# Three edits in the opening stage of a retention and mixture-of-experts kernel: two weight splits on another engine, a scaling moved up in a queue, a score step moved down

## The chip, the cores and the metric

The kernel runs on one core of a Trainium2 chip. The metric is the device time of one execution in microseconds (us). Five engines take part, each with its own queue that it works through in order: TensorE (PE in the rows; its weight loads are PEld), VectorE (DVE), ScalarE (ACT), GpSimd (POOL) and SyncE (SP), which only issues DMAs here.

## The reference

```python
scores = scale * np.matmul(q, k.transpose(0, 1, 3, 2))      # 4 batches, 8 heads, 576 tokens, 64 wide
gamma = 1.0 - 2.0 ** (-5.0 - np.arange(H))
Dmat = np.where(rel >= 0, gamma[:, None, None] ** rel, 0.0) # rel = i - j
x = np.matmul(scores * Dmat, v)                             # retention, no softmax
h = x @ w_in                                                # 2304 tokens, 512 -> 2048
x = (h / (1.0 + np.exp(-1.702 * h))) @ w_out                # dense layer, 2048 -> 512
# then a router picks one of 8 experts per token by cosine similarity,
# and the token goes through relu(x @ w1[e]) @ w2[e], times its gate
```

All arrays are float32. `w_in` and `w_out` arrive as 64-bit numbers and are turned into float32 in the kernel.

## The kernel before, in words

**Retention (functions inside `attention_`).** The 32 pairs of a batch and a head are taken two heads at a time: 16 "rows" bp, four to a batch (bp 0 to 3 are batch 0, bp 8 to 11 batch 2). The first 512 tokens of a row are worked in four chunks of 128, with a carried state between chunks; the last 64 tokens are the row's "end" and are worked by functions of their own. The tables `tb`/`tbs` hold powers of gamma. `decay` scales a row's keys in place (L335, on DVE for the rows of `DVE_ROWS = (0, 2, 7, 8, 9)`, else on POOL). For batches 2 and 3 it also scales the row's queries in place on POOL (L339) and, for the batch's first row, the end queries of all its four rows in one instruction (L342, tile `more`). `state` makes the carried state (PE L351, then ACT L352), `scores` and `masks` the chunk scores (PE L313, DVE L329), `scores_end` the scores of the ends of the rows in its list (PE L319, then DVE L322), `carried`, `ends_out` and `chunk` the outputs (PE L365, L373 and L375, L383), `keep` and `kept_out` move outputs from PSUM (DVE L404 for odd rows of the last two batches), `make_lows` splits the results of batches 0 and 1 for the next stage (POOL L433).

The rows are walked in groups, `[0], [1, 2], [3, 4], ... [13, 14], [15]`, numbered k = 0 to 8. In iteration k, `rows` is the group itself, `nxt` the next one, whose states and scores are prepared, and `then` the one after it, whose keys are scaled. Before the change the scaling of `then` stands at the head of the iteration for rows on POOL and at its tail for rows of `DVE_ROWS`; a row's query scaling stands with its key scaling. So the end queries of batch 2 (first row 8) are scaled at the tail of iteration 2, and those of batch 3 (first row 12) in the middle of the head of iteration 4. PE reads the end queries of row 8 in `scores_end(nxt)` of iteration 3.

**Weights of the dense layer (`convert`).** A unit u is the weights of 128 hidden columns; there are 16. For each, ACT takes the magnitude (L168), DVE works on bits (L181, L183, L191, L196), ACT makes the high half (L171) and a subtraction makes the low half (`low(u)`, L175): on POOL for units 0 and 1, on DVE for the others. PE's matmuls use both halves. `convert` is a generator: each `yield` gives the cost of the instruction in front of it, and `pull(us)` runs the generator until its budget is used up, an overdraft being taken from the next pull:

```python
while us > 0 and k < len(bg):
    cost = next(bg[k], None)
    ...
        us -= cost
debt.append(min(us, 0.0))
```

During retention there are nine pulls of 0.9 (one in iteration 5, three each in 6 and 7, two in 8), then one of 2.4, then one of 2.6 inside each step of the dense layer's first two blocks. The order of DVE's queue follows from these budgets alone.

**Dense layer.** Blocks of 384 tokens go through the 16 units; blocks 0 and 1 are interleaved, so unit f is used in steps 2f and 2f + 1. A step i is `layer1` (PE L566, 12 matmuls into one of two PSUM tiles `h`), then `swish`: ACT L597, DVE L599, ACT L600, the step's pull, DVE L604; and `layer2` (PE L577, 9 matmuls) of step i - 2. L599 frees the PSUM tile, so `layer1` of step i + 2 waits for L599 of step i, and the second matmul of `layer2` for L604.

After the two blocks come four more dense blocks with the router in between, then the experts. `fill_slots` (POOL L1003 and L1004) stands in POOL's queue behind retention and behind the two low halves.

Of the kernel before, what the change touches and what calls it, by code (L numbers as in the profile page):

```python
# [10 lines left out]
F32 = mybir.dt.float32  # L11
# [4 lines left out]
ALU = mybir.AluOpType  # L16

P = 128
B, H, S, HD = 4, 8, 576, 64
NPAIR = H // 2  # L20
NCH = 4
TAIL = S - NCH * P
# [35 lines left out]
AQ, AK, AV, AW = NCH * P, 2 * NCH * P, 3 * NCH * P, 4 * NCH * P  # L58
TQ, TV, TAW = TAIL, 2 * TAIL, 3 * TAIL
# [18 lines left out]
def retention_moe_kernel(  # L78
# [18 lines left out]
    PE, ACT, DVE, POOL, SP = nc.tensor, nc.scalar, nc.vector, nc.gpsimd, nc.sync  # L97
# [6 lines left out]
    c = pool.tile([P, CU], F32, name="c")  # L104
# [17 lines left out]
    units = {}  # L122
# [4 lines left out]
    def new_unit(u):  # L127
        s = u if u < NF1 else (u - NF1) % RING
        units[u] = unit_tile(f"unit{u}", [P, 2, 1024], F32R, HELD + s)
        return units[u]  # L130
# [14 lines left out]
    def load_due():  # L145

        if st.get("loaded"):
            while due:
                load_wd(due.pop(0))

    def flush(*keys):
        for k in keys or list(later):
            if k in later:
                later.pop(k)()

    def convert():

        words = [pool.tile([P, 1024], I32, tag="stg", bufs=2, name=f"ca{k}") for k in range(2)]

        def word(u):  # L160

            if u == 3 and len(words) == 2:
                t = pool.tile([P, 2, 1024], I32, tag="tab", bufs=2, name="ca")
                words.extend((t[:, 0, :], t[:, 1, :]))
            return words[u % 2 if u < 3 else (2, 3, 1, 0)[(u - 3) % 4]]

        def magnitude(u):
            ACT.activation(word(u).bitcast(F32), stg["d", u][:, :, 1].bitcast(F32), AF.Abs)  # L168

        def high(u):  # L170
            ACT.copy(new_unit(u)[:, 0, :], word(u).bitcast(F32))  # L171

        def low(u):
            flush(("high", u))
            (POOL if u < 2 else DVE).tensor_tensor(units[u][:, 1, :], word(u).bitcast(F32), units[u][:, 0, :].bitcast(F32), ALU.subtract)  # L175

        magnitude(0)
        for u in range(NF1):
            a = word(u)
            flush(("mag", u))  # L180
            DVE.tensor_scalar(a.bitcast(F32), a.bitcast(F32), 2.0**-15, CLAMP_HI, ALU.max, ALU.min)  # L181
            yield 0.67
            DVE.tensor_scalar(a, a, 3, 0x3FFFFFF8, ALU.logical_shift_left, ALU.bitwise_and)  # L183
            yield 0.67
            d = stg.pop(("d", u))
            if 0 < u < 4:
                low(u - 1)
                yield 1.22 if u > 2 else 0.1
            if u + 1 < NF1:
                later["mag", u + 1] = lambda u=u: magnitude(u + 1)  # L190
            DVE.scalar_tensor_tensor(a, d[:, :, 1], -0x40000000, a, ALU.bitwise_and, ALU.bitwise_or)  # L191
            yield 1.22
            if u > 3:
                low(u - 1)
                yield 1.22
            DVE.scalar_tensor_tensor(a, d[:, :, 0], 29, a, ALU.logical_shift_right, ALU.bitwise_or)  # L196
            if u + NWD < NF1:
                due.append(u + NWD)
                load_due()
            later["high", u] = lambda u=u: high(u)  # L200
            yield 1.22
        low(u)
        yield 0.1

# [35 lines left out]
    def attention_(psum):  # L240
# [5 lines left out]
        row = [place[i] for i in range(NBUF)] + [place[i] for i in order[2:]]  # L246
# [3 lines left out]
        tbs = tb[:, TX:n].rearrange("p (n w) -> p n w", w=TW)  # L250
# [3 lines left out]
        tl = [t[:, NPAIR * TAW * i : NPAIR * TAW * (i + 1)].rearrange("p (n w) -> p n w", w=TAW) for t in (ends, more) for i in range(2)]  # L254
# [42 lines left out]
        def idle(n, w=64):  # L297
            for _ in range(n):
                PE.matmul(warm[:w, :P], ones[:, :w], ones, start=True, stop=True)
# [15 lines left out]
        def scores_end(rows):  # L315
            for k, bp in enumerate(rows):
                e = tl[bp // NPAIR][:, bp % NPAIR, :]
                for r in heads:
                    PE.matmul(sct[r, TAIL * k : TAIL * (k + 1)], e[r, :TQ], e[r, TQ:TV], start=True, stop=True)  # L319
            for k, bp in enumerate(rows):  # L320
                g = tbs[:, bp % NPAIR, TE : TE + 1]
                DVE.scalar_tensor_tensor(pre[bp % 4], sct[:, TAIL * k : TAIL * (k + 1)], g, tri_end, ALU.mult, ALU.mult)  # L322
# [8 lines left out]
        def decay(bp):  # L331
            if bp < NBP:
                kd = row[bp][:, AK:AV].rearrange("p (c e) -> p c e", e=HD)
                dec = tbs[:, bp % NPAIR, TK:TS]
                (DVE if bp in DVE_ROWS else POOL).tensor_tensor(kd, kd, dec.unsqueeze(2).to_broadcast(kd.shape), ALU.mult)  # L335
                b, pair = divmod(bp, NPAIR)
                if b > 1:
                    qd = row[bp][:, AQ:AK].rearrange("p (c q) -> p c q", q=P)
                    POOL.tensor_tensor(qd, qd, tbs[:, pair, :P].unsqueeze(1).to_broadcast(qd.shape), ALU.mult)  # L339
                    if pair == 0:  # L340
                        qe = tl[b][:, :, TQ:TV]
                        POOL.tensor_tensor(qe, qe, tbs[:, :, :TAIL], ALU.mult)  # L342

        def state(bp, ch):
            t = row[bp]
# [12 lines left out]
        def carried(bp):  # L358
            t, kv = row[bp], kvs[bp % 2]
            new_out(bp)  # L360
            for ch in range(1, NCH):
                for r in heads:
                    o = st["o", bp][r, P * ch : P * (ch + 1)]
                    first = ch == 1 and bp > 0
                    PE.matmul(o, kv[r, 64 * (ch - 1) : 64 * ch], t[r, AQ + P * ch : AQ + P * (ch + 1)], start=first, stop=True, skip_group_check=not first)  # L365
# [28 lines left out]
        def keep_end(bp):  # L394
            x, o = kept_in(bp)[:, NCH * P :], st.pop(("ot", bp))
            if bp // NPAIR > 1:
                ACT.copy(x, o)
            else:
                DVE.tensor_tensor(x, o, tbs[:, bp % NPAIR, :TAIL], ALU.mult)
# [31 lines left out]
        def make_lows(b):  # L431
            while lows and lows[0][0] <= b:
                POOL.tensor_tensor(*lows.pop(0)[1:], ALU.subtract)  # L433
# [27 lines left out]
        for k, rows in enumerate(groups):  # L461
            nxt, then = (groups + [[], []])[k + 1 : k + 3]
            for bp in then:
                if bp > 2 and bp not in DVE_ROWS:
                    decay(bp)
            for bp in rows:
                carried(bp)
            ends_out(rows)
            scores_end(nxt)
            for bp in rows:  # L470
                keep_end(bp)
            if k > 5:
                yield False
            if nxt:
                scores(nxt[0])
            if k == 0:
                decay(2)
                masks(nxt[0])
                keep(0)
                for ch in range(NCH):  # L480
                    for bp in nxt:
                        state(bp, ch)
                    if ch == 1:
                        scores(nxt[1])
                        masks(nxt[1])
                    else:
                        idle(4)
            else:
                if nxt:
                    masks(nxt[0])  # L490
                values(rows, nxt)
            for bp in rows:
                if ("o", bp) in st:
                    kept_out(bp)
            make_lows(0 if k < 6 else 1)
            for bp in rows:
                if bp in WD_AT:
                    load_wd(WD_AT.index(bp))
                if bp in follows:
                    load(follows[bp])  # L500
                if follows.get(bp) == NBP - 1:

                    st["loaded"] = True
                    SP.dma_start(c[:, :CET], cst[:, :CET])
                    SP.dma_start(c[:, CET : CET + KD * E], embt)
                    uf = pool.tile([P, P], F32, tag="cvb", bufs=1, name="uf")
                    SP.dma_start(uf, cst[:, CU:CSL])
                    load_due()
            if k > 5:
                yield True  # L510
            for bp in nxt[1:] if k else []:
                scores(bp)
                masks(bp)
            for bp in then:
                if bp > 2 and bp in DVE_ROWS:
                    decay(bp)
            if 4 < k < 8:
                yield True
# [627 lines left out]
    for i in range(nd - 1):  # L1146
# [22 lines left out]
        if i >= LAG:  # L1169
            dense2(i - LAG)  # L1170
            u = i - LAG - (nd - NF1)
# [203 lines left out]
```

## Time and profile before

| | |
|---|---|
| median of three runs | 726.77 us (725.94 to 726.87) |
| the profiled execution | 727.92 us, of which the span shown is 726.1 us |
| PE busy | 706.9 us, 97% of the span |
| DVE busy | 458.3 us, 63% |
| ACT busy | 307.2 us, 42% |
| POOL busy | 207.2 us, 29% |

The span runs from the first to the last instruction in the record; 1.8 us of the execution lie around it. PE is busy nearly throughout, so the time is found in the places where it is not, or where its clock is not full.

### The profile page before, as it was taken

Reading aid. Unit: us, or ns where it says so; the run is one execution under the profiler, and the core shown is the slowest. Engines: PE = TensorE matmul, PEld = TensorE weight load, DVE = VectorE, ACT = ScalarE, POOL = GpSimd, SP = SyncE. Lnnn points to the kernel's source line nnn. Section 1 sums busy time; section 2 is a strip of 40 time slices with the busy share of each in tenths; the row PEclk is TensorE's granted clock in tenths of the full one; section 3 lists DMA queues with packets and bytes.
Section 4 is the critical chain, followed back from the end, with each engine's and each line's share of the span. In section 5 each row is a group of like instructions: output and inputs, shape, how many; then the busy total and the mean of one; then the engine's idle time right before and its main releaser. Section 6 shows DMA issues by size and latency. Waiting matters only on the chain. (4 is left out here: it accounts for less than half of the span.)

```text
span 726.1 us, 13167 instructions
## 1 busy us (share of the span) xinstructions
PE 706.9 (97%) x4903; PEld 657.3 (91%) x4903; DVE 458.3 (63%) x1034; ACT 307.2 (42%) x598; POOL 207.2 (29%) x195
## 2 busy tenths in 40 slices
PE   8999799999999999999999999999999999999995
PEld 7888699899899899899999889989999999999994
DVE  3668998888535887665477368656563553563561
ACT  2435354454345332332332244343444545555542
POOL 0673100000000221220111101224346546566553
PEclk9999899999999999999999999999999999999998
DMA  8997999000310013200400221144678879987861
GB/s 335 417 365 287 387 346 354 11 1 1 112 66 2 0 48 85 87 1 1 132 0 1 88 88 58 59 142 126 205 207 261 225 239 259 245 255 241 265 186 62
DMA packets 53156, 113.41 MB, mean 156 GB/s; under 512 B 8146, under 2 KB 29138, under 8 KB 48992
## 3 DMA queue, kind: packets, MB, share of 16 engines
q1 hardware_dynamic: 49744, 102.55, 43.6%
q0 software_dynamic: 3200, 9.46, 3.7%
q8 instruction: 39, 0.64, 0.4%
q10 hardware_dynamic: 144, 0.52, 0.2%
q14 instruction: 29, 0.24, 0.1%
HBM read 84.67 MB, written 28.17 MB: 155 GB/s over the span
## 5 line engine op out<-in xcount | busy, mean ns | idle before, releaser
L566 PE MATMUL h<-x,unit 128*128 128x384 f32 x1152 | 219.4, 339 | 3.5 <-DVE g0t L599 3.5
L566 PEld LDWEIGHTS h<-x,unit 128*128 128x128 f32 x1152 | 206.2, 189 | 12.2 <-DVE g0t L599 3.8
L222 POOL TENSOR_TENSOR unit<-we,unit 128x512 fp32r<-128x512 f32 x64 | 102.3, 1605 | 118.7 <-ACT unit L220 99.3
L566 PE MATMUL eh<-xt,unit 128*128 128x336 f32 (+6 forms) x672 | 102.1, 300 | 0.3 <-DVE eg54l L611 0.2
L566 PEld LDWEIGHTS eh<-xt,unit 128*128 128x128 f32 x672 | 95.4, 188 | 0.9 <-DVE eg54l L611 0.5
L221 DVE TENSOR_TENSOR unit<-we,unit 128x512 fp32r<-128x512 f32 x64 | 56.1, 877 | 59.2 <-ACT unit L220 58.7
L673 DVE CUSTOM_DVE_ANT_0 dj<-xr,en 128x512 bf16<-128x512 f32 x120 | 78.0, 696 | 0.0
L220 ACT CAST unit<-we 128x1024 fp32r<-128x1024 f32 x64 | 66.8, 1046 | 25.5 <-DMA we<-we 25.4
L639 POOL TENSOR_TENSOR enrm<-scr,c 128x8 f32<-128x8 f32 x1 | 1.7, 1687 | 142.0 <-ACT ej L644 142.0
L352 ACT ACTIVATE ends<-s,tb 128x64 f32<-128x64 f32 x64 | 17.4, 311 | 36.8 <-PE s L351 33.8
L616 POOL DMA_INDIRECT out<-y,idx x24 | 24.0, 1000 | 31.2 <-ACT y L839 20.6
L616 POOL DMA_INDIRECT xs<-xr,slot x18 | 19.4, 1077 | 39.1 <-DVE xr L748 35.7
L733 POOL TENSOR_TENSOR cum<-cum,oh_all 128x8 bf16<-128x8 bf16 x18 | 4.8, 265 | 67.2 <-PE rk L726 52.4
L539 POOL TENSOR_TENSOR x<-x0s,x 128x768 fp32r<-128x768 f32 x3 | 6.1, 2031 | 48.6 <-ACT x L538 48.6
L175 DVE TENSOR_TENSOR unit<-ca,unit 128x1024 fp32r<-128x1024 f32 x14 | 17.1, 1220 | 4.3 <-ACT unit L171 4.3
L191 DVE SCALAR_TENSOR_TENSOR ca<-wd,ca 128x1024 int32<-128x1024 int32 x16 | 19.6, 1222 | 0.3
L329 DVE SCALAR_TENSOR_TENSOR pr<-sc,tb 128x512 f32<-128x512 f32 x22 | 15.5, 745 | 6.7 <-PE sc L313 6.7
L196 DVE SCALAR_TENSOR_TENSOR ca<-wd,ca 128x1024 int32<-128x1024 int32 x16 | 19.5, 1219 | 0.1
L313 PE MATMUL sc<-row 64*128 64x128 f32 x256 | 18.8, 285 | 0.6 <-DMA row<-att 0.6
L839 ACT ACTIVATE y<-y,gate 128x512 f32<-128x512 f32 (+7 forms) x21 | 14.3, 713 | 10.9 <-DMA y<-yd 9.7
L335 POOL TENSOR_TENSOR row<-row,tb 128x512 f32<-128x512 f32 x11 | 11.5, 1044 | 24.8 <-DMA row<-att 13.2
L168 ACT ACTIVATE ca<-wd 128x1024 f32<-128x1024 f32 x16 | 18.3, 1147 | 0.0
(1312 smaller groups left out, 1543.7 us busy)
## 6 DMA issues: line engine op xcount, KB each, us to landing
we<-we SPq DMA_DIRECT2D x64, 512.0 KB, 4.5
wd<-wd SPq DMA_DIRECT2D x16, 1024.0 KB, 11.1
row<-att SPq DMA_DIRECT2D x14, 1024.0 KB, 13.2
xs<-fill SPq DMA_DIRECT2D x22, 257.0 KB, 10.8
xrow<-xr SPq DMA_DIRECT2D x18, 257.0 KB, 4.0
y<-yd SPq DMA_DIRECT2D x7, 512.0 KB, 4.7
x0d<-x0f SPq DMA_DIRECT2D x4, 768.0 KB, 11.3
x0s<-x0d SPq DMA_DIRECT2D x8, 384.0 KB, 6.7
```

The source lines that it names most:

```text
L168: ACT.activation(word(u).bitcast(F32), stg["d", u][:, :, 1].bitcast(F32), AF.Abs)
L175: (POOL if u < 2 else DVE).tensor_tensor(units[u][:, 1, :], word(u).bitcast(F32), units[u][:, 0, :].bitcast(F32), ALU.subtract)
L191: DVE.scalar_tensor_tensor(a, d[:, :, 1], -0x40000000, a, ALU.bitwise_and, ALU.bitwise_or)
L196: DVE.scalar_tensor_tensor(a, d[:, :, 0], 29, a, ALU.logical_shift_right, ALU.bitwise_or)
L220: ACT.copy(w[:, 0, :], t)
L221: DVE.tensor_tensor(w[:, 1, :512], t[:, :512], w[:, 0, :512].bitcast(F32), ALU.subtract)
L222: POOL.tensor_tensor(w[:, 1, 512:], t[:, 512:], w[:, 0, 512:].bitcast(F32), ALU.subtract)
L313: PE.matmul(scs[j][:, P * ch : P * (ch + 1)], t[r, P * ch : P * (ch + 1)], t[r, AQ + P * ch : AQ + P * (ch + 1)], start=True, stop=True)
L352: ACT.activation(kvs[bp % 2][:, 64 * ch : 64 * ch + 64], s, AF.Copy, scale=tbs[:, bp % NPAIR, TS + ch : TS + ch + 1])
L566: PE.matmul(h, w[:, a, P * dc : P * (dc + 1)], xt[:, b, dc, :n], start=k == 0, stop=k == len(terms) - 1)
L616: i = POOL.indirect_dma_start(out=dst[:, :], out_offset=bass.IndirectOffsetOnAxis(ap=rows, axis=0), in_=src, in_offset=None, bounds_check= ...
L673: DVE.tensor_tensor_reduce(junk, r[:, :D], en[e // 4][:, e % 4, :], 1.0, 0.0, ALU.mult, ALU.add, dots[:, E * k + e : E * k + e + 1])
```

## The change

The low halves of units 0 and 1 move from POOL to DVE, and their cost for the pulls becomes 1.22 in place of 0.1. `decay` is cut into three: key scaling stays where it was, the end queries of a batch are scaled at the head of the iteration before all else, and a row's queries are scaled at the head of the iteration whichever engine scales its keys. `scores_end(nxt)` of iteration 0 (rows 1 and 2) moves from in front of that iteration's scores and states to behind them.

```diff
         def low(u):
             flush(("high", u))
-            (POOL if u < 2 else DVE).tensor_tensor(units[u][:, 1, :], word(u).bitcast(F32), units[u][:, 0, :].bitcast(F32), ALU.subtract)
+            DVE.tensor_tensor(units[u][:, 1, :], word(u).bitcast(F32), units[u][:, 0, :].bitcast(F32), ALU.subtract)
...
             if 0 < u < 4:
                 low(u - 1)
-                yield 1.22 if u > 2 else 0.1
+                yield 1.22
...
                 (DVE if bp in DVE_ROWS else POOL).tensor_tensor(kd, kd, dec.unsqueeze(2).to_broadcast(kd.shape), ALU.mult)
-                b, pair = divmod(bp, NPAIR)
-                if b > 1:
-                    qd = row[bp][:, AQ:AK].rearrange("p (c q) -> p c q", q=P)
-                    POOL.tensor_tensor(qd, qd, tbs[:, pair, :P].unsqueeze(1).to_broadcast(qd.shape), ALU.mult)
-                    if pair == 0:
-                        qe = tl[b][:, :, TQ:TV]
-                        POOL.tensor_tensor(qe, qe, tbs[:, :, :TAIL], ALU.mult)
+
+        def decay_ends(bp):
+            b, pair = divmod(bp, NPAIR)
+            if b > 1 and pair == 0:
+                qe = tl[b][:, :, TQ:TV]
+                POOL.tensor_tensor(qe, qe, tbs[:, :, :TAIL], ALU.mult)
+
+        def decay_queries(bp):
+            b, pair = divmod(bp, NPAIR)
+            if b > 1:
+                qd = row[bp][:, AQ:AK].rearrange("p (c q) -> p c q", q=P)
+                POOL.tensor_tensor(qd, qd, tbs[:, pair, :P].unsqueeze(1).to_broadcast(qd.shape), ALU.mult)
...
             for bp in then:
+                decay_ends(bp)
+            for bp in then:
                 if bp > 2 and bp not in DVE_ROWS:
                     decay(bp)
+                decay_queries(bp)
             for bp in rows:
                 carried(bp)
             ends_out(rows)
-            scores_end(nxt)
+            if k:
+                scores_end(nxt)
...
                         idle(4)
+                scores_end(nxt)
             else:
```

## Rows read from the trace of the kernel before

**Rows 1.** Windows: stretch; its length, busy PE, PEld, DVE, ACT, POOL; granted clock; DMA.
```profile
38.60:41.90 3.30, 3.30 (x40) 3.30 (x42) 1.95 (x3) 1.06 (x4) 3.30 (x4) 0.50 1.02 422
84.00:89.00 5.00, 4.96 (x14) 4.35 (x15) 3.37 (x5) 2.88 (x4) 0.00 (x0) 0.50 1.01 426
150.00:200.00 50.00, 50.00 (x253) 45.28 (x252) 36.34 (x49) 21.43 (x34) 0.00 (x0) 1.00 0.13 44
```

**Rows 2.** PE's timeline, iterations 2 to 4: start, length, instruction, idle before.
```profile
27.76 0.40 PE L319 MATMUL sct<-ends 64*64 64x64 f32 x8
...
35.17 0.28 PE L319 MATMUL sct<-ends 64*64 64x64 f32 x4
37.15 0.33 PE L319 MATMUL sct<-more 64*64 64x64 f32 x4 [1.69 <-POOL more L342]
...
38.50 0.68 PE L351 MATMUL s<-row 128*64 128x64 f32 x8
...
46.11 0.40 PE L319 MATMUL sct<-more 64*64 64x64 f32 x8
```

**Rows 3.** POOL's timeline from 33 to 37 us.
```profile
33.22 1.55 POOL L433 TENSOR_TENSOR x<-x,x 128x384 fp32r<-128x384 f32 x2 [2.63 <-ACT x L423]
...
35.96 1.13 POOL L342 TENSOR_TENSOR more<-more,tb 128x256 f32<-128x256 f32 x1
```

**Rows 4.** SP's issue of batch 2's ends, and that DMA's time to landing.
```profile
15.55 0.33 SPq L269 DMA_DIRECT2D more<-tails  x1
...
more<-tails SPq DMA_DIRECT2D x1, 384.0 KB, 14.4
```

**Rows 5.** DVE's timeline: key scaling of row 2, and of rows 7 and 8.
```profile
13.49 0.68 DVE L335 TENSOR_TENSOR row<-row,tb 128x512 f32<-128x512 f32 x1
...
34.77 2.87 DVE L335 TENSOR_TENSOR row<-row,tb 128x512 f32<-128x512 f32 x2
```

**Rows 6.** Timeline of POOL and PE in iteration 1, row 4.
```profile
20.81 1.04 POOL L335 TENSOR_TENSOR row<-row,tb 128x512 f32<-128x512 f32 x1 [1.65 <-DMA row<-att]
...
21.91 0.34 PE L351 MATMUL s<-row 128*64 128x64 f32 x4 [0.26 <-POOL row L335]
```

**Rows 7.** PE's timeline from 74 to 104 us.
```profile
74.03 0.87 PE L365 MATMUL ao<-row,ends 64*64 64x128 f32 x12 [1.63 <-DVE x0f L404]
...
76.08 4.46 PE L566 MATMUL h<-x,unit 128*128 128x384 f32 x24
84.03 4.21 PE L566 MATMUL h<-x,unit 128*128 128x384 f32 x12 [3.48 <-DVE g0t L599]
...
91.12 2.25 PE L566 MATMUL h<-x,unit 128*128 128x384 f32 x12
...
103.66 2.27 PE L566 MATMUL h<-x,unit 128*128 128x384 f32 x12
```

**Rows 8.** POOL's timeline: the low halves of units 0 and 1.
```profile
68.42 2.35 POOL L175 TENSOR_TENSOR unit<-ca,unit 128x1024 fp32r<-128x1024 f32 x1 [9.08 <-ACT unit L171]
77.58 2.39 POOL L175 TENSOR_TENSOR unit<-ca,unit 128x1024 fp32r<-128x1024 f32 x1 [6.81 <-ACT unit L171]
```

**Rows 9.** DVE's and ACT's timelines from 68 to 88 us.
```profile
68.86 2.47 DVE L181 TENSOR_SCALAR ca<-ca 128x1024 f32<-128x1024 f32 x1
...
73.29 0.68 DVE L404 COPY x0f<-ao 128x512 f32<-128x512 f32 x1
...
77.62 3.37 DVE L183 TENSOR_SCALAR ca<-ca 128x1024 int32<-128x1024 int32 x1
...
83.42 0.55 DVE L599 SCALAR_TENSOR_TENSOR g0t<-g0t,h 128x384 f32<-128x384 f32 x1
...
84.42 1.14 ACT L168 ACTIVATE ca<-wd 128x1024 f32<-128x1024 f32 x1
85.60 0.69 DVE L181 TENSOR_SCALAR ca<-ca 128x1024 f32<-128x1024 f32 x1 [1.63 <-ACT ca L168]
...
86.93 1.22 DVE L175 TENSOR_TENSOR unit<-ca,unit 128x1024 fp32r<-128x1024 f32 x1
```

## The prediction

> **What bounds the kernel now.** I began with the busy times and the waits of PE, because PE is busy for nearly the whole span and its idle time is short enough to list. Behind the first hundred microseconds it hardly waits: from 150 to 200 us it is busy throughout, at full clock, with DVE and ACT well below and DMAs at 0.13 [rows 1]. Steps there follow each other at PE's pace, 4.18 us for a `layer1` and a `layer2` (three of them from 91.12 to 103.66 [rows 7]). So I take the rest of the kernel as rigid: what the opening saves arrives whole at the end. PE's timeline then shows three waits from 30 to 91 us: 1.69 for the scaled end queries of batch 2 [rows 2], 1.63 for a PSUM tile that DVE empties, and 3.48 for DVE's L599 of step 0 [rows 7]. The windows add that two of the three are paid twice. [...] I then followed each wait to its engine, in the timelines of POOL and DVE.
>
> **End queries earlier.** An ordinary iteration lasts 7.41 us from end scores to end scores (27.76 to 35.17), the one with the wait 10.94 (35.17 to 46.11) [rows 2]: 3.53 is lost, 1.69 in the wait and 1.84 in slow matmuls behind it. The wait is for L342, which runs on POOL from 35.96 to 37.09, behind two low halves and the query scaling L339 [rows 3]. After the change it is first in iteration 2. POOL is free from 30.59 (33.22 less the 2.63 idle [rows 3]) and the data landed at 29.95 (15.55 + 14.4 [rows 4]), so L342 should end near 31.8, 3.6 us before PE asks at 35.46. What is now queued behind it on POOL is the query scaling of row 8, then the two low halves of L433; those are read in the dense layer, some 40 us later. In iteration 4 L342 of batch 3 goes ahead of the scaling of rows 11 and 12, 1.13 us that their readers, an iteration later, don't notice. SP's queue has no DMA moved.
>
> What is late next is DVE's key scaling of rows 7 and 8. Two such instructions took 2.87 us, from 34.77, just when POOL went from L433 to L339 and L342; one alone took 0.68 [rows 5]. They would end at 37.64 again if POOL now worked beside them for as long (the rest of L433, then the queries of row 9), at 36.13 if it didn't. PE asks for row 8's states at about 36.8 (38.50 less 1.69 [rows 2]). So between 0 and 0.84 us of the 3.53 comes back as a new wait; I take 0.3, because less of POOL's work is left there than before. Gain 3.2, between 2.7 and 3.5.
>
> [...]
>
> **End scores of rows 1 and 2 behind their states.** These matmuls wait for a DMA in iteration 0, and PE can now go on with scores meanwhile. But in iteration 1 PE already waits 0.26 us for POOL's scaling of row 4, which starts when that row's DMA lands, at 20.81 [rows 6]. No edit brings that DMA forward, so what iteration 0 saves is spent there. Gain 0; at most the 0.26 that stands there now, and no loss, since DVE's part of the end scores is read only after the 24 matmuls of `carried`.
>
> **Low halves on DVE.** POOL's two splits take 2.35 and 2.39 us [rows 8], and beside each a DVE instruction is stretched: L181 to 2.47 and L183 to 3.37 [rows 9], where L181 at 85.60 takes 0.69. That is 1.78 and 2.68 of DVE's time, 4.46 together, against 2 x 1.22 (the same split on DVE, 86.93 [rows 9]) that the edit adds. POOL's fill instructions stood behind the second split and lengthened L183 with it; nothing now holds them back from the idle time after L433.
>
> The pulls also shift. With 1.22 for 0.1, the budgets of 0.9 hand out: end of iteration 5, L181 and L183 of unit 0; iteration 6, L191 and L196; iteration 7, L181 and L183 of unit 1, then low(0) with an overdraft that gives L191 to iteration 8's first pull and L196 to its second; the pull of 2.4, L181, L183 of unit 2 and low(1); step 0, L191 and L196; step 1, L181 and L183 of unit 3 and low(2). Conversion thus runs about one pull behind the old order.
>
> Now in the clock of the trace shown, before the 3.2 is taken off. (1) L404 of row 13 starts at 73.29 - 1.78 = 71.51 and ends at 72.19. PE is ready at 74.03 - 1.63 = 72.40, so that wait goes: 1.63. (2) `layer1` of step 0 starts at 76.08 - 1.63 = 74.45; steps 0 and 1 take 4.18, so PE is free at 78.63. (3) DVE behind 72.19 does low(0) 1.22, L191 and L196 2.43 (as from 80.99, the end of L183, to 83.42 [rows 9]), L404 of row 15 0.68, a small cast put at 0.2, L181 and L183 1.38, low(1) 1.22, L599 0.55: it ends at 79.87. PE waits 1.24 there, in place of 84.03 - 80.26 = 3.77. (4) `layer1` of step 2 ends at 81.96; L604 of step 0 ends at 79.87 + 2.43 + 0.55 = 82.85, so `layer2` of step 0 waits after its first matmul and ends at 84.7. (5) `layer1` of step 3 ends at 86.8. DVE has L599 of step 1 at 83.4, then ACT copies (0.5, estimated like L599) and takes the magnitude (1.14 [rows 9]) before L181 can start at 85.05; L183, low(2) and L604 put the end at 88.2. `layer2` of step 1 waits again and ends at 90.1.
>
> Before, that point (`layer1` of step 4) was 91.12 + 4.18 = 95.30, so the sum saves 5.2. The clock's part lies in it: from 84.03 to 91.12 a step took 7.09 in place of 4.18 [rows 7], and I hold that waits of about 1 us with full steps between leave the clock up, as the 1.63 at 72.40 did (24 matmuls behind it in 4.46, against 12 in 4.21 behind the 3.48 [rows 7]). Recorded lengths on DVE overlap: L181, L183 and the next start fit into 1.33 (85.60 to 86.93) where two lengths make 1.38, and more between independent ones; over a dozen instructions up to 1 us. With all of it the saving is 6.2. I take 6.0. The ceiling is a PE that never waits: 72.40 plus 2.05 plus six times 2.09 is 86.99, a saving of 8.3. From there on DVE needs 0.55 + 2.6 + 0.55 = 3.7 per step against PE's 4.18, and catches up.
>
> **Sum.** 3.2 + 0 + 6.0 = 9.2 us. The profiled execution took 727.92, so it would be 718.7 (span 716.9). The median of the runs is 1.15 below that execution; from 726.77 the forecast is 717.6.
>
> **Rivals.** (a) The clock falls again behind one of the three new waits (near 79, 82 or 87 us). For it: a wait of 1.69 was followed by a fall, one of 1.63 was not, so length alone doesn't decide. Against: none of mine is longer than 1.24. Price: the excess of that step, 7.09 - 4.18 = 2.9: 720.5. [...] (b) DVE's long L181 and L183 are not POOL's doing. Then the 4.46 stay, 2.44 are added on DVE, L599 of step 0 ends later and the low halves lose 2.4: 726.8 - 3.2 + 2.4 = 726.0. Against: L183's 3.37 begins and ends with POOL's work. (c) The end-query wait is only exchanged: 0.84 behind row 8's keys and the clock falls all the same (1.84), so that edit gives 0.85: 726.77 - 6.85 = 719.9. (d) Slower: the clock falls at the first new wait and DVE, behind with its conversion, makes PE wait in every following step, so that it stays down. At half clock PE loses half of the stretch; this decides from 18.4 us of it (twice 9.2), and 22 us would give 728.6. Against: before, the lower level lasted some 5 us behind a wait of 3.48 [rows 1], and DVE's 3.7 per step leaves PE without waits. (e) The opening is not rigid with the end, a DMA or the router absorbs it: 726.8. Against: PE's full windows.
>
> **How the numbers follow.** The forecast case has 0.80, with its own range from 714.7 (3.5 + 0.26 + 8.3 saved) to 718.9 (2.7 + 5.2). (a) 0.07, (b) 0.02, (c) 0.05, (d) 0.03, (e) 0.03. About 0.2% (1.5 us) is what a measurement of this kernel can tell from no change. Faster: forecast, (a) and (c), 0.92; same: (b) and (e), 0.05; slower: (d), 0.03. The range takes in the size errors of the forecast case and reaches to (a) and (c): 715.0 to 720.5.
>
> **What the profile would show.** Right: PE's end scores of row 8 without a wait and no clock at 0.50 near 39 us; end scores of iteration 4 near 42.8; a wait at row 4 grown to about 1 us; L181 and L183 at 0.69 throughout; `layer1` of step 2 near 76.7, behind a wait near 1 us; PE gapless from step 4. Wrong: clock 0.50 after 75 us; L335 of rows 7 and 8 still 2.87 with PE waiting for it; PE waits in steps 5 and later.

## The result, and the profile after

The changed kernel takes 718.39 us (median of four runs, 717.29 to 719.96) beside 726.36 for the kernel before (four runs, 725.65 to 726.87): ratio 0.9893, 95% interval 0.9871 to 0.9914. That is 7.8 us less (6.2 to 9.4) where 9.2 were forecast, and 718.39 where 717.6 was.

The execution that was profiled is the longest of the four: 719.96 us, span 718.1, against the 716.9 that the sum gave. Line numbers behind `decay` have moved: L341 scales end queries, L347 a row's queries, L356 is `state`, L438 `make_lows`, L576 and L587 are the two layers, L609 and L614 the old L599 and L604, and L620 the experts' activation (L610 before).

PE's timeline after, with its waits in brackets:

```profile
21.77 0.34 PE L356 MATMUL s<-row 128*64 128x64 f32 x4 [1.24 <-POOL row L335]
...
27.63 0.40 PE L319 MATMUL sct<-ends 64*64 64x64 f32 x8
...
35.03 0.28 PE L319 MATMUL sct<-ends 64*64 64x64 f32 x4
35.15 0.28 PE L319 MATMUL sct<-more 64*64 64x64 f32 x4
...
42.44 0.40 PE L319 MATMUL sct<-more 64*64 64x64 f32 x8
...
68.65 0.87 PE L370 MATMUL ao<-row,ends 64*64 64x128 f32 x12
...
70.71 4.43 PE L576 MATMUL h<-x,unit 128*128 128x384 f32 x24
75.77 2.35 PE L576 MATMUL h<-x,unit 128*128 128x384 f32 x12 [0.63 <-DVE g0t L609]
...
83.73 0.50 PE L587 MATMUL o<-unit,g1l 128*128 128x512 f32 x1 [0.65 <-DVE g1l L614]
...
94.24 2.27 PE L576 MATMUL h<-x,unit 128*128 128x384 f32 x12
```

The end scores of row 8 no longer wait, and iteration 4's follow at 42.44 where they were at 46.11 [rows 2]: 3.67 earlier, of which 0.14 is a start that was earlier already at the end scores of iteration 3 (35.03 for 35.17). The last wait of retention is gone, 3.48 in front of step 2 has become 0.63, and step 6 begins at 94.24 in place of 103.66 [rows 7]: 9.42 saved. So 3.53 come from the end queries and 5.75 from the low halves; the 0.14 is put down to neither. POOL and DVE of the same kernel show how:

```profile
20.68 1.04 POOL L335 TENSOR_TENSOR row<-row,tb 128x512 f32<-128x512 f32 x1 [1.65 <-DMA row<-att]
...
30.55 0.70 POOL L341 TENSOR_TENSOR more<-more,tb 128x256 f32<-128x256 f32 x1
...
33.72 2.05 POOL L438 TENSOR_TENSOR x<-x,x 128x384 fp32r<-128x384 f32 x2
```

```profile
34.64 1.68 DVE L335 TENSOR_TENSOR row<-row,tb 128x512 f32<-128x512 f32 x2
...
65.18 0.68 DVE L181 TENSOR_SCALAR ca<-ca 128x1024 f32<-128x1024 f32 x1
...
73.42 0.69 DVE L183 TENSOR_SCALAR ca<-ca 128x1024 int32<-128x1024 int32 x1
...
75.17 0.55 DVE L609 SCALAR_TENSOR_TENSOR g0t<-g0t,h 128x384 f32<-128x384 f32 x1
...
80.65 0.69 DVE L181 TENSOR_SCALAR ca<-ca 128x1024 f32<-128x1024 f32 x1 [1.60 <-ACT ca L168]
```

The end queries are scaled by 31.25, as soon as POOL is free. L181 and L183 take 0.69 where one of each took 2.47 and 3.37 [rows 9]. And L609 of step 0 ends at 75.72 where L599 ended at 83.97. The windows (stretch; its length, busy PE, PEld, DVE, ACT, POOL; granted clock; DMA) show a granted clock of 1.00 in each:

```profile
38.60:41.90 3.30, 3.30 (x60) 2.94 (x58) 2.15 (x4) 2.35 (x8) 2.02 (x4) 1.00 1.03 423
80.00:85.00 5.00, 4.35 (x23) 3.64 (x22) 4.32 (x6) 2.78 (x5) 0.00 (x0) 1.00 1.01 423
150.00:200.00 50.00, 50.00 (x253) 45.29 (x252) 33.51 (x47) 21.15 (x34) 0.00 (x0) 1.00 0.14 49
```

How far does the saving carry? ACT's instructions of the first and the last expert unit, and the cast of weights in front of unit 48, before and then after:

```profile
499.71 0.46 ACT L610 ACTIVATE eg0h<-eh 128x352 fp32r<-128x352 f32 x1
...
667.30 1.05 ACT L220 CAST unit<-we 128x1024 fp32r<-128x1024 f32 x1 [3.97 <-DMA we<-we]
...
711.14 0.39 ACT L610 ACTIVATE eg63h<-eh 128x264 fp32r<-128x264 f32 x1 [1.89 <-PE eh L566]
```

```profile
490.28 0.46 ACT L620 ACTIVATE eg0h<-eh 128x352 fp32r<-128x352 f32 x1
...
658.77 1.05 ACT L220 CAST unit<-we 128x1024 fp32r<-128x1024 f32 x1 [3.95 <-DMA we<-we]
...
703.16 0.39 ACT L620 ACTIVATE eg63h<-eh 128x264 fp32r<-128x264 f32 x1 [1.64 <-PE eh L576]
```

At the first expert unit 9.43 us are saved (499.71 - 490.28), at the last 7.98. Between them ACT waits at the cast L220 for a DMA of expert weights, 3.97 us before and 3.95 after. The length is the same, but the cast starts only 8.53 earlier (667.30 - 658.77), less than the 9.43 that the opening had saved. Behind it, PE's list of waits from 640 to 720 us (what waited for what; us in total, times, longest) has two that before has not:

```profile
PE eo L597 <- ACT unit L220: 1.0, 1, 1.0
PE eh L576 <- DVE eg48l L621: 0.6, 1, 0.6
```

Two questions follow. The profiled opening saved what was forecast, yet the medians differ by less. And the end of the kernel took back 1.5 us that the opening had saved.

### The profile page after: what moved, and what is told of

Same layout as the page of the kernel before. It is cut to its first block, busy times and chain, and to the rows that moved or that the text cites. A ratio compares the mean times of both kernels' runs of the same rounds, so it can differ in the third digit from the quotient of the medians.

```text
span 718.1 us, 13166 instructions
## 1 busy us (share of the span) xinstructions
PE 702.8 (98%) x4903; PEld 653.3 (91%) x4903; DVE 453.3 (63%) x1036; ACT 306.6 (43%) x598; POOL 204.9 (29%) x193
## 4 chain that ended last, share of the span: by engine, by line
PE 82%; DMA 8%; DVE 3%; issue 3%; SPq 2%; ACT 1%; POOL 1%; POOLq 0%; ACTq 0%; DVEq 0%
PE o L587 28%; PE h L576 27%; PE eh L576 10%; PE eo L597 9%; DMA row<-att 3%; DMA we<-we 2%; PE ao L388 2%; PE sc L313 2%; DMA yd<-yq 1%; DMA y<-yd 1%; PE ao L370 1%; PE s L356 1%; SPq L836 1%; ACT unit L220 1%; DVE unit L221 1%
## 5 line engine op out<-in xcount | busy, mean ns | idle before, releaser
L576 PE MATMUL h<-x,unit 128*128 128x384 f32 x1152 | 217.5, 337 | 0.6 <-DVE g0t L609 0.6
L576 PEld LDWEIGHTS h<-x,unit 128*128 128x128 f32 x1152 | 204.6, 188 | 9.2 <-DVE g0t L609 0.9
L576 PE MATMUL eh<-xt,unit 128*128 128x336 f32 (+6 forms) x672 | 102.2, 301 | 0.7 <-DVE eg48l L621 0.6
L576 PEld LDWEIGHTS eh<-xt,unit 128*128 128x128 f32 x672 | 95.4, 188 | 1.5 <-DVE eg48l L621 0.8
L221 DVE TENSOR_TENSOR unit<-we,unit 128x512 fp32r<-128x512 f32 x64 | 53.6, 838 | 62.6 <-ACT unit L220 58.6
L220 ACT CAST unit<-we 128x1024 fp32r<-128x1024 f32 x64 | 66.8, 1046 | 26.9 <-DMA we<-we 24.7
L175 DVE TENSOR_TENSOR unit<-ca,unit 128x1024 fp32r<-128x1024 f32 x16 | 19.5, 1221 | 3.1 <-ACT unit L171 3.1
L191 DVE SCALAR_TENSOR_TENSOR ca<-wd,ca 128x1024 int32<-128x1024 int32 x16 | 19.6, 1222 | 0.3
L817 ACT CAST xt<-tp 128x336 fp32r<-128x336 f32 (+6 forms) x28 | 11.1, 411 | 18.2 <-DVE tp L815 18.2
```

What stands on the lines that cost most here:

```text
L175: DVE.tensor_tensor(units[u][:, 1, :], word(u).bitcast(F32), units[u][:, 0, :].bitcast(F32), ALU.subtract)
L220: ACT.copy(w[:, 0, :], t)
L221: DVE.tensor_tensor(w[:, 1, :512], t[:, :512], w[:, 0, :512].bitcast(F32), ALU.subtract)
L576: PE.matmul(h, w[:, a, P * dc : P * (dc + 1)], xt[:, b, dc, :n], start=k == 0, stop=k == len(terms) - 1)
```

## The experiments

Each was run beside the kernel before on the same chip; us are worked out as one less the ratio, times the median of before beside it (726.02 to 726.18).

**The end and query scaling alone (e1).** The changed kernel with the two other edits undone:

```diff
-            DVE.tensor_tensor(units[u][:, 1, :], word(u).bitcast(F32), units[u][:, 0, :].bitcast(F32), ALU.subtract)
+            (POOL if u < 2 else DVE).tensor_tensor(units[u][:, 1, :], word(u).bitcast(F32), units[u][:, 0, :].bitcast(F32), ALU.subtract)
...
-                yield 1.22
+                yield 1.22 if u > 2 else 0.1
...
-            if k:
-                scores_end(nxt)
+            scores_end(nxt)
...
-                scores_end(nxt)
```

> Only the scaling moved up (L342 and L339 at the head of the iteration); low halves on POOL for units 0 and 1 and the end scores as before. Theory (the three edits add up, each where its wait stood): the 1.69 wait at row 8's end scores and the slow clock behind it go, 3.5 us, so 722.9. Rival 1 (the parts share one gain, since the later DVE chain absorbs an earlier PE): PE only waits longer for L599 of step 0, under 1.5 us, 725 or more. Rival 2 (a new wait for row 8's keys takes part of it): 723.7.

Ratio 0.9963 (0.9950 to 0.9977): 2.7 us saved (1.7 to 3.6). No wait for end queries; those of 1.6 for the PSUM tile and 3.5 for L599 of step 0 stand as before. The first rival (under 1.5) is out; the interval holds the theory's 3.5 as well as the second rival.

**The low halves alone (e2).** The kernel before with the first two hunks of the change:

```diff
-            (POOL if u < 2 else DVE).tensor_tensor(units[u][:, 1, :], word(u).bitcast(F32), units[u][:, 0, :].bitcast(F32), ALU.subtract)
+            DVE.tensor_tensor(units[u][:, 1, :], word(u).bitcast(F32), units[u][:, 0, :].bitcast(F32), ALU.subtract)
...
-                yield 1.22 if u > 2 else 0.1
+                yield 1.22
```

> Only the low halves of units 0 and 1 on DVE, with cost 1.22; the rest as before. Theory: the waits of 1.63 and 3.48 and the slow clock from 83 to 89 us go, three waits of 0.3 to 0.9 come, 5.75 us saved, so 720.6. Rival 1 (parts share one gain): all of the 8 us or none, 718.4 or 725. Rival 2 (DVE is only loaded more): 726 or above.

Ratio 0.9920 (0.9906 to 0.9934): 5.8 us saved (4.8 to 6.8), the size that the profile of after gave. Its PE timeline and its window hold the surprise:

```profile
37.01 0.33 PE L319 MATMUL sct<-more 64*64 64x64 f32 x4 [1.69 <-POOL more L342]
...
44.34 0.40 PE L319 MATMUL sct<-more 64*64 64x64 f32 x8
```

```profile
38.60:41.90 3.30, 3.30 (x72) 3.07 (x70) 2.65 (x4) 2.06 (x9) 3.30 (x4) 1.00 1.03 424
```

The wait of 1.69 is there to the hundredth, but the clock is 1.00 behind it, and the iteration lasts 9.31 (from 35.03) in place of 10.94. This edit touches nothing before 60 us. So the slow stretch of [rows 1] is not a fixed price of that wait.

The granted clock of whole runs points the same way. It is 1.00 from 100 to 640 us in the profiles of before and after, and 1.00 from 100 to 200 in those of e1 to e3 and e5 to e7, so where one run's mean is below another's, the opening (or the very end) is the likely place. Of e2's six runs, four have a mean of 0.996 and took 719.2 to 720.2 us; two have 0.994 and 0.993 and took 721.0 and 721.5. A fall of 3.3 us to 0.50 takes 0.0023 off the mean of 718 us (an estimate from [rows 1]), so the two look like runs that paid for the wait; where their clock was down is not on record.

**The end scores alone (e3).** The kernel before with the last two hunks of the change:

```diff
-            scores_end(nxt)
+            if k:
+                scores_end(nxt)
...
+                scores_end(nxt)
```

> Only the end scores of rows 1 and 2 behind their states. Theory: the wait for the DMA of the ends is exchanged for a longer one for row 4's keys (0.26 grows to 1.2), time as before, 726.4 within 0.3. Rival (the 0.74 is kept): 725.7.

Ratio 1.0017 (1.0003 to 1.0032): 1.2 us slower (0.2 to 2.3), which neither forecast holds. The profiled run, 725.02, was the shortest of its ten (up to 730.08) and shows nothing that costs this: the wait at row 4 is 0.71 (1.2 was forecast), the wait for end queries 1.69 with the clock up behind it (1.00 from 38.6 to 41.9). The longer runs have a lower clock: the mean of all ten is 0.9902, beside 0.9915 for the fifteen of the kernel before, and 0.0013 of 726 us is some 0.9 us. Why the clock was down more often, and where, is not on record.

**All but the end scores (e4).** The changed kernel with the diff of e3 reversed.

> The whole change without the move of the end scores of rows 1 and 2. Theory: as the changed kernel, 718.4 within 0.5. Rival (that move gives 0.74 or more when the others are there): 719.1 or more. In its trace I also look at the expert stage: by the theory that the 1.5 us lost there in the changed kernel are the chance timing of DMAs against ACT's queue, the loss between the fortieth expert unit and the end should differ from run to run, between 0 and 2 us; if it comes from the earlier opening, it should be near 1.5 here and smaller in the runs of the two single edits.

Ratio 0.9890 (0.9874 to 0.9905), as with the score step. The expert stage lost nothing here (8.52 us saved at its first unit, 8.60 at its last). But the profile shows a wait that the changed kernel did not have; POOL, DVE and PE in turn:

```profile
34.59 0.58 POOL L438 TENSOR_TENSOR x<-x,x 128x192 fp32r<-128x192 f32 x1
35.14 1.74 POOL L347 TENSOR_TENSOR row<-row,tb 128x512 f32<-128x512 f32 x1
```

```profile
34.63 1.10 DVE L335 TENSOR_TENSOR row<-row,tb 128x512 f32<-128x512 f32 x1
35.65 1.78 DVE L335 TENSOR_TENSOR row<-row,tb 128x512 f32<-128x512 f32 x1
```

```profile
37.53 0.34 PE L356 MATMUL s<-row 128*64 128x64 f32 x4 [0.75 <-PE s L356]
```

PE's 0.75 is put down to its own instruction in front, which had long ended; what was late is L335 of DVE, to 37.43. The two engines race, and 0.04 us decide: POOL's second subtraction of L438 starts at 34.59, DVE's first scaling at 34.63, and it is DVE's that is stretched (0.68 alone). In the changed kernel DVE was first by 0.04, and POOL's was stretched:

```profile
34.64 0.68 DVE L335 TENSOR_TENSOR row<-row,tb 128x512 f32<-128x512 f32 x1
34.68 1.08 POOL L438 TENSOR_TENSOR x<-x,x 128x192 fp32r<-128x192 f32 x1
```

Of the seven profiles with the end queries scaled at the head, the five in which DVE started first had no such wait (DVE's pair 1.68 to 1.80); e8 below had 0.22 (2.38) and this one 0.75. In all seven, the one of the two that started second took far longer than alone: DVE's scaling up to 1.78 us for 0.68, POOL's second subtraction 1.08 in the changed kernel for 0.58 here.

**Only the end queries at the head (e8).** The changed kernel with a row's query scaling back beside its key scaling:

```diff
                 if bp > 2 and bp not in DVE_ROWS:
                     decay(bp)
-                decay_queries(bp)
+                    decay_queries(bp)
...
                 if bp > 2 and bp in DVE_ROWS:
                     decay(bp)
+                    decay_queries(bp)
```

> The changed kernel with the query scaling L339 back beside each row's key scaling; only the end queries stay at the head of the iteration. Theory (the end queries are the whole gain of that edit): no wait at row 8's end scores, 718.4 within 0.6; in the trace L335 of rows 7 and 8 may be stretched by POOL as in the kernel without the score move, where it took 2.80 and PE waited 0.75. Rival (the queries had to move too): 720 or more.

Ratio 0.9895 (0.9879 to 0.9911), the same as the whole change. That edit's gain comes from the end queries; the order of the row's queries is worth nothing that was measured.

**Only the order of the conversion (e5).** The kernel before with the cost alone changed, so that POOL keeps both splits:

```diff
-                yield 1.22 if u > 2 else 0.1
+                yield 1.22
```

> The kernel before with only the pull cost of low(0) and low(1) raised to 1.22; both stay on POOL. It changes nothing but the order of DVE's queue: L191 and L196 of unit 2 move behind L599 of step 0. Theory (both halves of the edit are needed: POOL's splits stretch DVE, and the order puts 2.4 us of conversion in front of L599): L181 of unit 1 and L183 of unit 2 stay stretched (about 2.5 and 3.3 us), the 1.63 wait for L404 stays, the wait for L599 shrinks by 1.5 to 2.4 us, and PE is let go when POOL's low(1) ends; 722 to 724.5. Rival (the stretching by POOL is all): 726.2. Rival (the order is all): 720.4.

Ratio 0.9962 (0.9948 to 0.9976): 2.8 us saved (1.7 to 3.8). DVE, POOL and PE:

```profile
67.00 2.47 DVE L181 TENSOR_SCALAR ca<-ca 128x1024 f32<-128x1024 f32 x1
...
79.17 2.67 DVE L191 SCALAR_TENSOR_TENSOR ca<-wd,ca 128x1024 int32<-128x1024 int32 x1
```

```profile
66.56 2.35 POOL L175 TENSOR_TENSOR unit<-ca,unit 128x1024 fp32r<-128x1024 f32 x1 [8.73 <-ACT unit L171]
...
78.26 2.50 POOL L175 TENSOR_TENSOR unit<-ca,unit 128x1024 fp32r<-128x1024 f32 x1 [9.35 <-ACT unit L171]
```

```profile
72.16 0.87 PE L365 MATMUL ao<-row,ends 64*64 64x128 f32 x12 [1.63 <-DVE x0f L404]
...
75.10 5.47 PE L566 MATMUL h<-x,unit 128*128 128x384 f32 x26
80.81 2.03 PE L566 MATMUL h<-x,unit 128*128 128x384 f32 x10 [0.24 <-POOL unit L175]
```

The long instruction beside the second split was L183 before and is L191 here (it takes 1.22 elsewhere); the theory had expected L183 again. But here it comes behind L599 of step 0, and PE waits 0.24, for POOL's split, in place of 3.48 for L599. Not all of that is the order's doing: the clock was down behind the 1.63 (0.63 from 72 to 76.6), step 0 began 2.94 us behind the L365 shown in place of 2.05 [rows 7], and so PE came later to the wait. The first split still stretches L181, and the wait of 1.63 for L404 stays.

**Only the engine (e6).** DVE does all low halves, the cost stays at 0.1:

```diff
-            (POOL if u < 2 else DVE).tensor_tensor(units[u][:, 1, :], word(u).bitcast(F32), units[u][:, 0, :].bitcast(F32), ALU.subtract)
+            DVE.tensor_tensor(units[u][:, 1, :], word(u).bitcast(F32), units[u][:, 0, :].bitcast(F32), ALU.subtract)
```

> The kernel before with only the engine of low(0) and low(1) changed to DVE; their pull cost stays 0.1, so L191 and L196 of unit 2 stay in front of L599 of step 0. Theory: L181 and L183 take 0.69 each, the 1.63 wait goes, but PE still waits some 2.9 us for L599; DVE is then one pull further on, so the waits of steps 0 and 1 for L604 do not come. 721.0 if the clock stays up behind the 2.9, 723.0 if it falls. Rival (the stretching by POOL is all): 720.0.

Ratio 0.9979 (0.9964 to 0.9993): 1.5 us saved (0.5 to 2.6). PE's timeline:

```profile
81.38 3.66 PE L566 MATMUL h<-x,unit 128*128 128x384 f32 x12 [2.85 <-DVE g0t L599]
```

L181 and L183 take 0.69 and the wait for L404 is gone, but with the old budgets DVE works so much ahead of L599 that PE waits 2.85 there, and the clock falls behind it (0.52 from 82 to 84.7). The median, 724.31, is above the 723.0 forecast for that case, and one wait for L604 (0.56) came that the theory had not. Each half of the edit removes one of the two long waits and keeps the other. Together they gave 5.8; the two alone add up to 4.3, with about 1 of uncertainty each, so that they help each other beyond adding up is not shown.

**PE kept busy through the wait (e7).** The kernel before, with small matmuls into unused columns put in front of row 8's end scores:

```diff
+            if k == 3:
+                for _ in range(32):
+                    PE.matmul(sct[:64, 256 : 256 + P], ones[:, :64], ones, start=True, stop=True)
             scores_end(nxt)
```

> The kernel before, with 32 small matmuls into an unused part of the score tile put in front of row 8's end scores, so that PE works while it waits for the end queries; the wait itself ends when it ended. Theory (a fall of the clock behind the 1.69 us wait is a second price of it, paid in some executions): the fall in the next scores, 1.84 us, does not come in the profiled execution; iteration 3 lasts 9.1 to 9.4 us in place of 10.94, and the median falls by what share of the executions paid it, between 0 and 1.84 us (0.9 if half of them do). Rival (PE's idle time has nothing to do with that clock): iteration 3 still takes 10.9 in executions like that of before, and the median stays within 0.3 us.

```profile
35.08 1.97 PE L471 MATMUL sct<-ones 128*64 128x128 bf16 x32
...
44.44 0.40 PE L319 MATMUL sct<-more 64*64 64x64 f32 x8
```

The iteration lasts 9.36 and the clock from 38.6 to 41.9 is 1.00. Yet the ratio is 0.9999 (0.9988 to 1.0010): at most 0.9 us saved. So on average the runs of the kernel before pay at most half of the 1.84 behind that wait, if the small matmuls keep the clock up in all runs as in this one. Whether PE's idle time sets off the fall is not settled: of the five profiles with the wait and no matmuls in it (before, e2, e3, e5, e6), three have the clock up as well, and the medians fit none of the runs paying as well as nearly half of them. The mean clock leans to the theory, 0.9922 for the twelve runs with the small matmuls and 0.9911 for the seventeen without.

**The changed kernel again (r1).** No edit.

> The changed kernel, unaltered. Theory (what the opening saves is fixed, what the expert stage gives or takes is chance): 9.4 us saved at the first expert unit within 0.3, as in its first profile, and a change between the first expert unit and the end that may be anything from 2 us lost to 1 us gained, not the 1.5 lost again; median 717.5 to 718.5. Rival (the opening's shift sets the order of DMAs at the end): the same 1.5 lost at the same expert units, span 718.1.

718.71 us (717.06 to 719.64), ratio 0.9899 (0.9880 to 0.9918). ACT's first and last expert units in the profiled run, span 715.2:

```profile
489.99 0.46 ACT L620 ACTIVATE eg0h<-eh 128x352 fp32r<-128x352 f32 x1
...
700.32 0.39 ACT L620 ACTIVATE eg63h<-eh 128x264 fp32r<-128x264 f32 x1 [1.89 <-PE eh L576]
```

9.72 saved at the first expert unit (forecast 9.4 within 0.3), 10.82 at the last: this time the expert stage gave 1.1 where it had taken 1.5, with the same program. That is a little more than the 1 us allowed for, as the median is 0.2 above its bound. Over the profiles of all these kernels the time from the first expert unit to the end of the span, against before, ran from 1.4 lost to 1.2 gained, with no visible relation to how far the opening was ahead.

**The next magnitude ahead of the step's tanh (e9).** After the change DVE sat idle for 1.60 at 80.65, because ACT takes the next unit's magnitude only behind the step's copies. The changed kernel, with that magnitude moved up:

```diff
+        if work:
+            flush(*[k for k in later if k[0] == "mag"])
         ACT.activation(th, h, AF.Tanh, scale=0.851)
```

> The changed kernel with one thing more: a step's pending magnitude (ACT L168) goes to ACT in front of the step's tanh and not behind its copy. Theory (in step 1 DVE idles 1.6 us for that magnitude, which makes the wait for L604 of step 1): the idle 1.6 in front of L181 of unit 3 goes, the wait of 0.65 in step 1 with it, 0.9 to 1.3 us saved against the changed kernel, 717.3. Rival (the tanh behind the magnitude is late instead, or DVE's queue only fills with the next thing): no gain, 718.4.

Ratio 0.9884 (0.9867 to 0.9901), 717.37 us. DVE and PE:

```profile
78.62 0.69 DVE L181 TENSOR_SCALAR ca<-ca 128x1024 f32<-128x1024 f32 x1
```

```profile
92.80 2.27 PE L576 MATMUL h<-x,unit 128*128 128x384 f32 x12
```

The idle time and the wait of 0.65 behind it are gone, and step 6 starts 1.44 earlier than after, of which 0.35 stood already at step 2 (75.42 for 75.77). In the medians that is some 1 us which the intervals don't separate from the changed kernel.

**The same without the score step (e10).** The kernel of e9 with the diff of e3 reversed.

> The changed kernel with the next unit's magnitude put in front of each step's tanh on ACT, and with the end scores of rows 1 and 2 back in front of their states. Theory (the score step is worth nothing either way beside the other edits): 717.4 within 0.6, as with the score step. Rival (the score step helps or hurts by about a microsecond): 716.4 or 718.4.

718.42 us, ratio 0.9895 (0.9875 to 0.9915). From e4 to the changed kernel the score step went with 0.2 more, here with 1 less: neither is outside the intervals, and its worth beside the other edits stays at nothing that was measured.

## Why the prediction was right, and where its size was off

**End queries earlier.** The mechanism was right: POOL scales them by 31.25 (forecast 31.8), PE does not wait, the clock stays up, and iteration 4's end scores stand at 42.44 (forecast near 42.8). In the profiled execution the whole 3.53 was gained, with nothing of the 0.3 for rows 7 and 8. The mis-sized term is the 1.84 of slow matmuls in it. It was read from one execution and taken off the median, as though every execution paid it. Five profiled executions have the wait of 1.69 with PE idle through it: before and e6 show the fall (iteration 10.94 and 10.89), e2, e3 and e5 do not (9.31 each), and keeping PE busy in it (e7) lowers the median by 0.9 at most. Without the fall the edit is worth 9.31 - 7.41 = 1.9, and 1.9 + 5.8 = 7.7 is what the medians of the whole change show (7.8, and 7.3 in r1). Alone (e1) it gave 2.7, and that interval (1.7 to 3.6) holds the forecast 3.2 as well as 1.9: that not every execution pays the 1.84 is shown, by the three profiles without it; how much too much it was for a median is argued from e7 and stays open. That the profiled execution lay above the median was seen in the prediction, but the sum was carried over whole. Why the clock fell in two of the five executions and not in the other three, no run shows.

The new wait for DVE's key scaling stayed in its bounds: between 0 and the 0.84 of the upper end, with 0, 0.22 and 0.75 seen. But the reason for taking 0.3, that less of POOL's work is left there, did not decide it. POOL worked beside DVE throughout, and which of the two started first decided, by 0.04 us in e4 (DVE's pair 2.80) and in the changed kernel (1.68); that the changed kernel paid nothing is luck more than foresight.

One cost went unseen: at the head of iteration 4 POOL now waits 1.28 us for the DMA of batch 3's end queries (L341 starts at 41.22), with the key scalings of two rows queued behind it. PE has no wait from it.

**End scores behind the states.** Forecast 0, and beside the other edits nothing was measured. The wait at row 4 grew from 0.26 to 1.24, since its POOL instruction still starts when the DMA lands (20.68), and the end scores of iteration 2 start at 27.63 with the step and at 27.62 without (e4). Alone it measured 1.2 slower, which the bounds did not hold; its runs had a lower clock, and the cause of that is open.

**Low halves on DVE.** Forecast 6.0, measured 5.75 in the profile and 5.8 alone. The steps came as they were worked out: the wait for L404 gone; PE free at 75.14 (forecast 78.63, less the 3.67 that this execution was ahead: 74.96); L609 at 75.72 (76.20); step 4 at 85.67 (90.1 less 3.67: 86.43). The waits were smaller than forecast, 0.63 for 1.24 before step 2, because DVE's instructions overlap, as was allowed for (from 68.51, the end of L409, the old L404, to the end of L609 their lengths add up to 7.72 in 7.21 us), and the clock stayed up behind all of them (1.00 from 72 to 95 us). With the splits taken off POOL and nothing else changed (e6), L181 and L183 take 0.69, and in e5 another instruction, L191, is stretched beside a split: so rival (b) falls. The order, which the cost sets, saved 2.8 alone and the engine 1.5, with intervals that overlap. One sign failed in part: L183 of unit 0 took 0.96 in the changed kernel, beside POOL's L438, and not 0.69.

**The rest is rigid.** Right from step 6 to the expert stage, where the saving stays within 0.15 us, and then not quite: the expert stage adds or takes up to some 1.5 us from one execution to the next. In the first profile of the changed kernel the cast in front of unit 48 came forward by 8.53 where the opening had saved 9.43, and PE waited 1.0 and 0.6 behind it; in r1, which had no such waits, the stage gave 1.1. That the weights' DMAs decide is read from the waits; no run changed them.

**Rivals.** (a) and (d): no fall of the clock behind the new waits in either profile of the changed kernel (1.00 from 72 to 95 us in both). (c): the exchange of the wait occurs in one profile of seven, with 0.75 of the 0.84, and without the fall (8.36 from end scores to end scores, 35.02 to 43.38, beside 10.94). (e): partly, as above, with both signs.

## What to carry to other kernels

A wait of PE's may be paid a second time in slow matmuls, but behind the short wait here (1.69 us) two of five profiled executions paid it: before that price is taken off a median, look for it in more than one profile, compare the mean clock of the runs, or keep PE busy there and time it. A cost that a hand-written planner uses is part of the edit that moves the work: here the same engine change gives 1.5 us with the old cost and 5.8 with the new one. When an instruction on DVE looks several times too long (2.47 and 3.37 us for 0.69 here), look at what GpSimd does beside it before thinking of the instruction.

## What the runs showed of the hardware

- The same wait of PE, 1.69 us, behind the same work, was followed by a lower clock in two of five executions (0.50 in the kernel before and 0.62 in e6, from 38.6 to 41.9) and by a clock of 1.00 in three (e2, e3, e5). Behind the 1.63 of retention's last wait the clock was down in e5 (0.63 from 72 to 76.6) and up in the kernel before (1.00 from 74 to 78.6). Behind the longer wait in front of step 2 (3.48 us before, 2.85 in e6; in e1, e3 and e7 PE idled 3.48, 3.67 and 3.88 us from 72 to 84) it was down in all five executions that have it: 0.50 before (84 to 89), 0.57 in e1 and 0.70 in e3 (80 to 84), 0.52 in e6 (82 to 84.7), 0.61 in e7 (84 to 89).
- Of DVE's key scaling (L335) and the GpSimd instruction beside it, the one that started second was stretched, in eight profiles (before, after, r1, e1, e4, e8, e9, e10), with starts as little as 0.03 us apart (34.74 and 34.77 before): a DVE scaling to between 1.08 and 1.78 from 0.68, or GpSimd's pair of subtractions to between 1.99 and 2.07 from 1.54 or 1.55 (the second of them to 1.08 from 0.59). In the other five profiles DVE's pair took 2.86 to 2.88, beside 2.87 before. The stretch lies in the recorded length and not in a wait.
- The end-query scaling on GpSimd took 0.70 us beside DVE's L413 (30.67 in the changed kernel), which reads the PSUM tile `ao`, and 1.13 next to the key scaling [rows 3].
